# Rows of x sent straight to their expert's places, without a token table

## The chip, the cores and the metric

One core of a Trainium2 chip runs the kernel. It has five engines that run their own instruction lists in order: TensorE (matmuls), VectorE, ScalarE, GpSimd and SyncE (DMA issues only). The metric is the device time of one execution in microseconds (us), lower is better. The clock of TensorE is granted in two levels, 1.2 and 2.4 GHz; the profile gives the share of full speed in each stretch.

## What is computed

A linear attention (8 batches, 8 heads, 576 positions, 64 wide) feeds a mixture of experts with one expert for each token (4608 tokens, 512 wide, 8 experts, hidden width 1024).

```python
def _attn_ref(q, k, v):
    q_s = np.exp(q - np.max(q, axis=-1, keepdims=True))
    q_s = q_s / (np.sum(q_s, axis=-1, keepdims=True) + 1e-09)
    k_s = np.exp(k - np.max(k, axis=2, keepdims=True))
    k_s = k_s / (np.sum(k_s, axis=2, keepdims=True) + 1e-09)
    kv = np.einsum('bhsd,bhse->bhde', k_s, v)
    return np.einsum('bhsd,bhde->bhse', q_s, kv)
def _moe_ref(x, expert_emb, tau, w1, w2):
    # xn, en: rows of x and expert_emb divided by their norm
    logits = xn @ en.T / tau
    expert_idx = np.argmax(logits, axis=1)
    # gate_w: softmax of the logits at expert_idx
    for e in range(E):
        mask = expert_idx == e
        h = np.maximum(x[mask] @ w1[e], 0.0)
        out[mask] = gate_w[mask, None] * (h @ w2[e])
```

x is the attention's result with positions as rows and heads side by side.

## The kernel before

The work goes in four groups of two batches (g = 0 to 3; 1152 tokens, nine tiles of 128). A group's attention has named steps: loads `lk`, `lv`, `lq` (1152 KB each, two of each in a group, on SyncE's queue); the maximum over k (`mx`, `pT`, `mcol`, `mc`, `pB`, `mb`), subtraction `ks`, exponential `ke`; `von` and `vc` copy v beside a column of ones on ScalarE; `kv0` to `kv3` multiply k and v on TensorE; `rs`, `kvx`, `kvd`, `pkT`, `kvT`, `pG`, `cG` make the matrix that gives x and the expert logits at once. For q there are the maximum `qm`, the subtraction `qs` on GpSimd, and for each tile the transposes `pE`, exponential `ec`, matmul `px`, and `ra`, `rr`, `xm`, `lm`, `sq`, which leave x in SBUF and the logits.

Routing goes in five parts, a to e: group 0 in two (a: five tiles, b: four), the others whole. `r`, `pr`, `s` (prefix z for b) find each token's expert and its place among that expert's tokens (`posu`); `gA` to `gE` give the gate. Each expert owns 4608 places. A table in DRAM of 8 bytes for each place holds the token's number and gate: it is first filled with an out-of-range number (`cP`, L266 to L268: a memset on GpSimd, a DMA on SyncE ahead of all loads), and each tile's 128 entries are scattered into it (`sc0` to `sc8`, an indirect DMA on GpSimd, L705). x goes to DRAM in token order by two stores for each group (`st0`, `st1`, L603), and its first five tiles once more for slot 0 (`sta`, L615).

Tokens are processed in slots, each for one expert. Six early slots (256 tokens) run between the attention steps: slots 0 and 1 after parts a and b, slots 2 to 5 after part c, planned by `ya`, `yb`, `yc` on VectorE. The rest are late slots (384 tokens), planned by `lp` and run in a loop under conditions that the device evaluates. A slot loads its stretch of the table (`ix`, SyncE, L931), masks numbers past its end (`im`, VectorE, L1073), gathers its rows of x by these numbers (`xg`, an indirect DMA on GpSimd for every 128 rows, L936), transposes them (`x..p`, `x..h`, `x..l`), runs the two layers (`pa`, `pb`, `hh`, `hl`, `po`, `ob`; each operand split into a high and a low part, so three matmuls for each product) and scatters the result to `out` (`od`, L1018). Slot 0 doesn't read the table: `first_ids` (`fo`, `fp`, `fi`) makes its numbers by a one-hot comparison on VectorE and a matmul, and it gathers from the copy of L615.

`ORDER` is one list of all steps, written out: each engine issues its instructions in this order and waits where an operand is late. `room` and `load` give the tiles for k, v, q: group 0 has its own on the left; later groups have one each for k0, k1, ve0, ve1 and two in turn for v and q on the right. The tile of x holds first q less its maximum, then x.

Of the kernel before, what the change touches and what calls it, by code (L numbers as in the profile page):

```python
# [12 lines left out]
I32 = mybir.dt.int32  # L13
# [16 lines left out]
KX = D + E + 1  # L30
TS = 3
T = TS * P
CAP = N
SENT = E * CAP
TROWS = SENT + T
# [25 lines left out]
PAD_LEFT, PAD_RIGHT = 88, 176  # L61
# [10 lines left out]
cP.0 enL.0 lk0.0 lk1.0 lv0.0 lq0.0 lq1.0 kvP.0 lv1.1 cV.0 lk0.1 von0.1 lv1.0 von1.1 von1.0 von0.0 lk1.1 lv0.1 mx00.0  # L72
mx01.0 enA.0 mx02.0 mx03.0 pT0.0 mx10.0 mcol0.0 mx11.0 mc0.0 pB0.0 enV.0 vc0.0 ks00.0 enP.0 enC.0 ke00.0 mx12.0
qm0.0 kv0.0 mx13.0 kv1.0 qs00.0 qm1.0 pT1.0 qs01.0 vc1.1 mcol1.0 qs11.0 mc1.0 lq0.1 pB1.0 qs10.0 ks10.0 vc1.0 pE0.0
mx00.1 pE2.0 mx01.1 pE1.0 mx02.1 ke10.0 mx03.1 mx10.1 ec2.0 kv2.0 mx11.1 ec1.0 ec0.0 mx12.1 pT0.1 kv3.0 vc0.1
mcol0.1 mx13.1 pT1.1 left.4 rs.0 mcol1.1 kvd.0 lq1.1 kvx.0 mc0.1 pkT.0 qm0.1 pB0.1 kvT.0 mb0.1 pG.0 mc1.1 ks01.1
pB1.1 cG.0 pE3.0 ks10.1 px1.0 px2.0 qs00.1 ec3.0 pE5.0 ra1.0 ra2.0 pE6.0 rr1.0 ke10.1 rr2.0 xm1.0 pE4.0 ks00.1 lm2.0
xm2.0 lm1.0 px3.0 sq1.0 qm1.1 px0.0 ec4.0 qs01.1 ra3.0 pE7.0 ke00.1 rr3.0 xm3.0 qs10.1 lv1.2 lm3.0 ec6.0 px4.0 ec7.0
pE8.0 ra0.0 ra4.0 rr0.0 qs11.1 sq3.0 rr4.0 xm0.0 ec5.0 xm4.0 sq2.0 lm4.0 sta.0 lm0.0 px6.0 sq0.0 r0.0 lv0.2 px7.0
sq4.0 r1.0 st0.0 r2.0 ra6.0 pE0.1 gA.0 r3.0 ec8.0 rr6.0 r4.0 pE2.1 ra7.0 xm6.0 ec0.1 pE1.1 r5.0 sq6.0 rr7.0 pr.0  # L80
lm6.0 xm7.0 px8.0 s0.0 sq7.0 lm7.0 s1.0 px5.0 gB.0 ec1.1 s2.0 gC.0 ra8.0 ra5.0 rr8.0 gD.0 s3.0 rr5.0 ec2.1 s4.0
# [10 lines left out]
w2h03.4 pb03.4 mcol1.2 st0.1 hl02.4 sq4.1 px7.1 rr5.1 hh03.4 xm5.1 w2l03.4 w202.4 x1p1.4 ra7.1 hl03.4 sq5.1 x1p0.4
rr7.1 pB0.2 lm5.1 x1h1.4 lm7.1 px8.1 xm7.1 x1h0.4 w200.4 mb0.2 x1l1.4 px6.1 sq7.1 ks01.2 x1l0.4 ra8.1 ra6.1 rr8.1
pa13.4 mc1.2 rr6.1 lm8.1 xm6.1 xm8.1 sq6.1 pa10.4 ks00.2 lm6.1 st1.1 sq8.1 r0.1 w2h02.4 pb13.4 r1.1 w2h00.4 gA.1
w2l02.4 pB1.2 pb10.4 ke00.2 w2l00.4 ks10.2 po00.4 qs00.2 ke10.2 r2.1 qs11.2 kv0.2 qs10.2 ob00.4 pa11.4 qs01.2 lv1.3
po01.4 od00.4 gB.1 lv0.3 r3.1 gC.1 r4.1 gD.1 r5.1 gE.1 pb11.4 hh10.4 ob01.4 hl10.4 kv1.2 hh13.4 od01.4 hh11.4 hl13.4
# [5 lines left out]
xm1.2 sq0.2 qm0.3 sq1.2 ec5.2 w1h12.4 im2.4 w1l12.4 pT0.3 xg2.4 w2h11.4 px7.2 im3.4 pT1.3 w110.4 mcol0.3 ra7.2 pE4.2
ob11.4 rr7.2 mcol1.3 px5.2 mc0.3 xm7.2 w2l11.4 pB0.3 lm7.2 sq7.2 pE3.2 ec4.2 px6.2 ra5.2 od11.4 mc1.3 pE8.2 rr5.2
w210.4 mb0.3 lm5.2 ra6.2 xm5.2 x2p1.4 ec3.2 ks00.3 rr6.2 px4.2 sq5.2 lm6.2 xm6.2 x2p0.4 x2h1.4 ra4.2 px3.2 x2l1.4
x2h0.4 ks01.3 rr4.2 ec8.2 pE2.2 x2l0.4 ix4.4 sq6.2 pB1.3 lm4.2 xm4.2 pa23.4 w2h10.4 ks10.3 ec2.2 xg3.4 px8.2 sq4.2
pb23.4 ra3.2 w1h10.4 w2l10.4 pa21.4 ke10.3 w1l10.4 w212.4 pa22.4 im4.4 w213.4 rr3.2 hh23.4 lm3.2 xm3.2 pb21.4 ra8.2
# [12 lines left out]
s1.3 x5l1.4 s2.3 s3.3 lp0.3 s4.3 lp1.3 s5.3 lp2.3 s6.3 lp3.3 sc7.3 lp4.3 lp5.3 lp6.3 lp7.3 sc0.3 lp8.3 lp9.3 x5p0.4
lp10.3 ob40.4 lp11.3 sc4.3 lp12.3 lp13.3 x5h0.4 po41.4 lp14.3 lp15.3 sc6.3 x5l0.4 lp16.3 sc8.3 lp17.3 lp18.3 lp19.3  # L120
lp20.3 sc2.3 lp21.3 lp22.3 lp23.3 lp24.3 od40.4 lp25.3 lp26.3 lp27.3 lp28.3 sc3.3 lp29.3 lp30.3 lp31.3 sc5.3 ob41.4
od41.4 sc1.3 right.4
# [4 lines left out]
def attention_moe(ctx, tc, q, k, v, emb, tau, w1, w2, out):  # L127
# [30 lines left out]
    early_rows = wk.tile([P, EARLY_J, DM], F32, tag="xge", bufs=1, name="xge")  # L158
# [13 lines left out]
    x_scr = dram.tile([N, DM], F32, name="x_scr")  # L172

    NA = ROUTES["a"][2]
    x_a = dram.tile([P * NA, DM], F32, name="x_a")
    table = dram.tile([TROWS, 2], I32, name="table")

# [9 lines left out]

    row = const.tile([P, NT, 2], I32, name="row")
# [52 lines left out]
    def const_steps():  # L241
        s = {}

        def cP():
# [8 lines left out]
            for i in range(2):  # L253
                POOL.iota(part_i[:, :, i], [[0, NA]], base=0, channel_multiplier=(NA - 1, 1)[i])
# [72 lines left out]
    def room(side, what, shape):  # L327

        return att[side].tile(shape, F32, tag=what, name=what)
# [881 lines left out]
```

## Time and profile before

| | us |
|---|---|
| median of 3 runs (lowest, highest) | 649.75 (648.42, 651.2) |
| profiled execution | 644.16 |
| its span, first to last instruction | 642.3 |
| TensorE busy (matmuls) | 561.1 |
| VectorE, ScalarE, GpSimd busy | 336.0, 280.5, 202.4 |
| stores of x for one group; the copy for slot 0 | 1280 KB and 1024 KB; 1280 KB |
| bytes moved by DMA; read from, written to HBM | 109.78 MB; 89.71 MB, 21.04 MB |

The profiled execution is one run with the hardware profiler on. Busy times overlap, so they don't add up to the span. The number behind an instruction in the rows below is its idle time before it, and after the arrow what ended that.

### The profile page before, as it was taken

What the parts mean: (1) busy time and instruction counts of PE and PEld (TensorE: products, weight loads), DVE (VectorE), ACT (ScalarE), POOL (GpSimd) and SP (SyncE); (2) the same over time, 40 slices, a digit from 0 to 9 for tenths busy, and PEclk for the clock granted to TensorE, in tenths of its full rate; (3) what the DMA queues carried; (4) which work ended last, traced back from release to release, by engine and by line L of the source; (5) the groups of instructions that cost most, each with busy time, mean ns of one, the idle gap of its engine ahead of it and who ended that gap; (6) DMA issues with size and microseconds to landing.
All of it is one profiled execution on the core that took longest, in us unless ns stands there. A gap on an engine that the chain in (4) does not pass through costs nothing. (4 is left out here: it accounts for less than half of the span.)

```text
span 642.3 us, 13299 instructions
## 1 busy us (share of the span) xinstructions
PE 561.1 (87%) x5178; PEld 501.3 (78%) x5178; DVE 336.0 (52%) x569; ACT 280.5 (44%) x420; POOL 202.4 (32%) x194
## 2 busy tenths in 40 slices
PE   0467658996989895999799999999999999999995
PEld 0356547885869784888699989889989898989894
DVE  4977548972968822262245365652536252544440
ACT  2568345732568143221345355552534353434440
POOL 3417260965163724126320302203030211213111
PEclk9997768997979996999899999999999999999999
DMA  6984992845846100321794567755464555554100
GB/s 214 391 299 175 330 282 58 311 165 167 275 135 247 51 19 2 132 84 34 262 294 129 167 191 238 229 166 186 134 194 134 181 180 164 181 182 139 63 23 29
DMA packets 65859, 109.78 MB, mean 171 GB/s; under 512 B 10702, under 2 KB 35310, under 8 KB 64624
## 3 DMA queue, kind: packets, MB, share of 16 engines
q1 hardware_dynamic: 58144, 89.74, 42.9%
q0 software_dynamic: 7552, 18.92, 8.6%
q8 instruction: 51, 0.84, 0.6%
q14 instruction: 32, 0.26, 0.1%
q10 hardware_dynamic: 80, 0.02, 0.0%
HBM read 89.71 MB, written 21.04 MB: 172 GB/s over the span
## 5 line engine op out<-in xcount | busy, mean ns | idle before, releaser
L1018 POOL DMA_INDIRECT out_dram<-ob,ix x38 | 39.4, 1037 | 288.6 <-ACT ob L1016 248.2
L993 PE MATMUL ph<-x,w1h 128*128 128x384 f32 (+1 forms) x320 | 102.2, 319 | 2.2 <-ACT ob L1016 1.2
L995 PE MATMUL ph<-x,w1l 128*128 128x384 f32 (+1 forms) x320 | 102.1, 319 | 0.0
L994 PE MATMUL ph<-x,w1h 128*128 128x384 f32 (+1 forms) x320 | 102.0, 319 | 0.0
L961 DVE TENSOR_TENSOR w2l<-r,w2h 128x1024 fp32r<-128x1024 f32 x44 | 54.6, 1242 | 73.6 <-ACT w2h L959 73.6
L1011 PE MATMUL po<-w2h,h_l 128*128 128x512 f32 x224 | 88.8, 396 | 0.1
L1012 PE MATMUL po<-w2l,h_l 128*128 128x512 f32 x224 | 87.7, 391 | 0.0
L1013 PE MATMUL po<-w2h,h_l 128*128 128x512 f32 x224 | 87.6, 391 | 0.0
L1016 ACT ACTIVATE ob<-po,ix 128x512 f32<-128x512 f32 x38 | 26.2, 688 | 128.5 <-PE po L1013 64.4
L999 DVE SCALAR_TENSOR_TENSOR h_l<-ph,h_l 128x768 fp32r<-128x768 f32 (+1 forms) x44 | 37.9, 861 | 75.2 <-ACT h_l L997 73.1
L961 DVE TENSOR_TENSOR w1l<-r,w1h 128x1024 fp32r<-128x1024 f32 x48 | 56.8, 1219 | 28.5 <-ACT w1h L959 25.3
L997 ACT ACTIVATE h_l<-ph 128x768 fp32r<-128x768 f32 (+1 forms) x44 | 32.3, 734 | 87.2 <-issue 64.0
L993 PEld LDWEIGHTS ph<-x,w1h 128*128 128x128 f32 x320 | 60.4, 189 | 3.3 <-ACT ob L1016 1.6
L994 PEld LDWEIGHTS ph<-x,w1h 128*128 128x128 f32 x320 | 60.5, 189 | 0.3
L995 PEld LDWEIGHTS ph<-x,w1l 128*128 128x128 f32 x320 | 60.5, 189 | 0.0
L993 PE MATMUL ph<-x_e,w1h 128*128 128x256 f32 x192 | 57.4, 299 | 1.0 <-ACT et L550 0.7
L994 PE MATMUL ph<-x_e,w1h 128*128 128x256 f32 x192 | 55.5, 289 | 0.2
L995 PE MATMUL ph<-x_e,w1l 128*128 128x256 f32 x192 | 55.4, 288 | 0.2 <-issue 0.2
L959 ACT CAST w2h<-r 128x1024 fp32r<-128x1024 f32 x48 | 50.1, 1043 | 4.2 <-ACT ob L1016 1.2
L959 ACT CAST w1h<-r 128x1024 fp32r<-128x1024 f32 x48 | 48.4, 1051 | 5.6 <-DMA r<-in_moe_w_dram 5.6
L1013 PEld LDWEIGHTS po<-w2h,h_l 128*128 128x128 f32 x224 | 42.3, 189 | 9.0
L1011 PEld LDWEIGHTS po<-w2h,h_l 128*128 128x128 f32 x224 | 42.4, 189 | 8.8 <-issue 0.3
(274 smaller groups left out, 1057.7 us busy)
## 6 DMA issues: line engine op xcount, KB each, us to landing
r<-in_moe_w_dram SPq DMA_DIRECT2D x96, 512.0 KB
k<-in_k_dram SPq DMA_DIRECT2D x8, 1152.0 KB
v<-in_v_dram SPq DMA_DIRECT2D x8, 1152.0 KB
q<-in_q_dram SPq DMA_DIRECT2D x8, 1152.0 KB
x_scr<-x SPq DMA_DIRECT2D x4, 1280.0 KB
x_scr<-x SPq DMA_DIRECT2D x4, 1024.0 KB
x_a<-x SPq DMA_DIRECT2D x1, 1280.0 KB
out_dram<-ob,ix POOLq DMA_INDIRECT x38
```

The lines of the kernel that those rows point to most:

```text
L959: ACT.copy(hi, src)
L961: eng.tensor_tensor(lo, src, hi.bitcast(F32), ALU.subtract)
L993: PE.matmul(o, w1h[c][:, d, fs], xh[:, d, :n], start=d == 0, stop=False)
L994: PE.matmul(o, w1h[c][:, d, fs], xl[:, d, :n], start=False, stop=False)
L995: PE.matmul(o, w1l[c][:, d, fs], xh[:, d, :n], start=False, stop=d == NC1 - 1)
L997: ACT.activation(hh[c][:, :, :n], ph[:, :, :n], AF.Relu)
L999: DVE.scalar_tensor_tensor(hl[c][:, :, :n], ph[:, :, :n], 0.0, hh[c][:, :, :n].bitcast(F32), ALU.max, ALU.subtract)
L1011: PE.matmul(po, hh[c][:, u, ts_], w2h[c][:, u, :], start=c + u == 0, stop=False)
L1012: PE.matmul(po, hh[c][:, u, ts_], w2l[c][:, u, :], start=False, stop=False)
L1013: PE.matmul(po, hl[c][:, u, ts_], w2h[c][:, u, :], start=False, stop=c + u == NC2 // 2)
L1016: ACT.activation(ob, po, AF.Copy, scale=ix[:, j, 1:2].bitcast(F32))
L1018: ins = POOL.indirect_dma_start(out, bass.IndirectOffsetOnAxis(ap=ix[:, j, 0:1], axis=0), ob, None, bounds_check=N - 1, oob_is_err=False,)
```

## The change

The table, its first filling, the stores of x in token order, the copy for slot 0 and `first_ids` are removed. A row of x in SBUF gets two words more (`DX` = 514): the token's number (`xi`, one iota for each group) and its gate (written by `gE`). `sc` now scatters these whole rows of 2056 bytes, 128 at a time, to their expert's places in DRAM (`x_by_e`), as many scatters as before. Since a slot's tokens then lie one after another, the plan computes row numbers from a start and a count (`place`, `over`), the slot gathers with them directly, and two VectorE instructions (`numbers`, step `im`) take number and gate out of the gathered rows. The late plan spreads its starts and counts over partitions with a matmul (`lq`) and four steps (`lr`). Gathers and scatters are declared independent where a scatter follows a gather; a gather still waits for the scatters before it.

k, v, ve, q of groups 1 to 3 share six places in turn (`RING`, the one whose last user stands earliest in `ORDER`), and for groups 2 and 3 q less its maximum has two of these places (`qd`) instead of x's tile. `ORDER` is written anew: its beginning, the stretch around slot 0's gather (before, `xg0.4` stood behind four scatters of part a) and that of group 1's scatters now read

```
cP.0 enL.0 lk0.0 lk1.0 lq1.0 lv0.0 lq0.0 xi.0 lv1.0 cV.0 kvP.0 lk0.1 lv1.1 von0.0 von1.0 xi.1 lk1.1 lv0.1 mx00.0
...
ya11.0 w1h02.4 zs3.0 lm2.1 zs4.0 sc0.0 mx10.2 zs5.0 w1h00.4 mx11.2 yb0.0 w1l00.4 zs6.0 w103.4 yb1.0 sc8.0 rr0.1
xm2.1 lm0.1 sc7.0 px7.1 sq2.1 xm0.1 qm0.2 px3.1 sq0.1 sc5.0 ra7.1 ec8.1 sc6.0 ra3.1 pE5.1 ec6.1 qm1.2 w1h03.4 pE4.1
w1l03.4 xg0.4 mx12.2 w203.4 rr7.1 mx13.2 xm7.1 hroom.4 lm7.1 sq7.1 yb2.0 px8.1 mcol0.2 yb3.0 mc0.2 w1l02.4 pT1.2
ra8.1 ec4.1 rr8.1 w2h03.4 w200.4 pB0.2 im0.4 mcol1.2 lm8.1 x0p0.4 mb0.2 w2l03.4 xm8.1 mc1.2 x0p1.4 x0h0.4 rr3.1
...
s6.1 yc3.1 sc3.1 mx10.3 lq1.3 yc4.1 mx11.3 sc8.1 pa12.4 ob01.4 yc5.1 mx12.3 hh11.4 sc6.1 pb13.4 yc6.1 hl11.4 od01.4
yc7.1 mx13.3 w110.4 pb12.4 sc1.1 hh13.4 w111.4 yc8.1 yc9.1 yc10.1 hl13.4 sc7.1 pT0.3 hh12.4 yc11.1 pa10.4 mcol0.3
sc2.1 hl12.4 mc0.3 qm1.3 sc0.1 pT1.3 pkT.2 sc4.1 pb10.4 kvT.2 sc5.1 mcol1.3 pB0.3 hh10.4 pG.2 mc1.3 hl10.4 mb0.3
w1h10.4 pB1.3 ks00.3 cG.2 po10.4 ks10.3 w1h11.4 ks01.3 ke10.3 xi.2 w1l11.4 xg2.4 ke00.3 pE1.2 w1l10.4 w211.4 pE3.2
```

The diff's core:

```diff
+DX = DM + 2
-SENT = E * CAP
-TROWS = SENT + T
+ROWS = E * CAP
+RING = 6
-    x_scr = dram.tile([N, DM], F32, name="x_scr")
-    x_a = dram.tile([P * NA, DM], F32, name="x_a")
-    table = dram.tile([TROWS, 2], I32, name="table")
+    x_by_e = dram.tile([ROWS, DX], I32, name="x_by_e")
...
-            oob = wk.tile([P, TROWS * 2 // P], I32, tag="lh", bufs=1, name="oob")
-            POOL.memset(oob, OOB)
-            SP.dma_start(table.rearrange("(p f) o -> p (f o)", p=P), oob)
...
+    def room(g, what, shape, users):
+        if not g:
+            return att["left"].tile(shape, F32, tag=what, name=what)
+        done = {i: max((emitted[x] for x in old), default=-1) for i, old in enumerate(ring) if emitted.keys() >= set(old)}
+        i = min(done, key=done.get)
+        ring[i] = [f"{x}.{g}" for x in users]
...
         def qs(u, i):
-            if u + i == 0:
-                buf["x", g] = room("right" if g else "x0", "x", [P, GT, DM])
+            if i == 0 and g >= 2:
+                s["qd", u] = room(g, f"qd{u}", [P, GT, 2, P], [f"pE{j}" for j in range(GT)])
+            elif i == 0:
+                s["qd", u] = x_of(g)[:, :, :DM].rearrange("p j (b c x) -> p b j c x", b=2, c=2)[:, u]
...
+        def xi():
+            POOL.iota(x_of(g).bitcast(I32)[:, :, DM], [[1, GT]], base=2 * g * S, channel_multiplier=GT)
...
-            DVE.reciprocal(row[:, cs, 1].bitcast(F32), col("gs"))
+            DVE.reciprocal(buf["x", g][:, j0:j1, DM + 1], col("gs"))
...
             ins = POOL.indirect_dma_start(
-                table,
+                x_by_e,
                 bass.IndirectOffsetOnAxis(ap=posu[:, c : c + 1], axis=0),
-                row[:, c, :],
+                buf["x", g][:, j].bitcast(I32),
                 None,
...
+            tc.declare_no_dep(ins.ins, group="gather", reason="rows that no part routed before has")
...
+            lambda: DVE.scalar_tensor_tensor(place, number_q, val[:, 1:2], over, ALU.add, ALU.max),
...
+        def spread():
+            b["t"] = ps.tile([P, 2, n], F32, tag="t", name="spread")
+            PE.matmul(b["t"], ones[:n, :], start_count, start=True, stop=True)
...
+        chain(NG - 1, "lr", [
+            lambda: DVE.tensor_tensor(over, number_n, b["ct"], ALU.is_ge),
+            lambda: DVE.tensor_scalar(over, over, float(OOB), None, ALU.mult),
+            lambda: DVE.tensor_tensor(place, number_n, b["st"], ALU.add),
+            lambda: DVE.tensor_tensor(place, place, over, ALU.max),
+        ])
...
-        def places():
...
-            SP.dma_start(ix[:, :nt], table[ds(st, nt * P), :].rearrange("(j p) o -> p j o", p=P).bitcast(U32))
         def tokens():
             for j in range(nt):
...
+                ins = POOL.indirect_dma_start(
+                    xg[:, j].bitcast(I32), None, x_by_e, bass.IndirectOffsetOnAxis(ap=place[:, i, j : j + 1], axis=0),
+                    bounds_check=ROWS - 1, oob_is_err=False,
                 )
+        def numbers():
+            DVE.tensor_tensor(ix[:, :, 0], xg.bitcast(U32)[:, :, DM], over[:, i], ALU.max)
+            DVE.tensor_copy(ix[:, :, 1].bitcast(F32), xg[:, :, DM + 1])
...
-    first_ids()
```

## Rows read from the trace of the kernel before

**Rows 1.** Stretches of the span: busy time of each engine, granted clock, DMA share, GB/s.
```profile
0.00:20.00 20.00, 1.94 (x8) 1.07 (x8) 10.55 (x24) 5.80 (x7) 5.62 (x41) 1.00 0.71 249
20.00:40.00 20.00, 9.66 (x209) 8.37 (x212) 16.67 (x18) 11.71 (x10) 8.68 (x4) 1.00 1.06 391
80.00:100.00 20.00, 11.77 (x141) 9.68 (x138) 9.46 (x32) 8.95 (x15) 10.31 (x10) 0.59 1.00 269
...
0.00:320.00 320.00, 248.07 (x3459) 215.72 (x3460) 190.07 (x431) 143.00 (x256) 141.31 (x140) 0.90 0.54 181
320.00:640.00 320.00, 313.01 (x1720) 285.58 (x1719) 145.93 (x138) 137.49 (x165) 61.08 (x54) 1.00 0.51 162
```

**Rows 2.** SyncE's DMA queue, 0 to 8 us: start, us, line, tensors, [idle before].
```profile
5.21 0.39 SPq L268 DMA_DIRECT2D table<-oob  x1
5.65 1.03 SPq L341 DMA_DIRECT2D k<-in_k_dram  x2
```

**Rows 3.** ScalarE's DMA queue, 0 to 8 us.
```profile
0.82 1.58 ACTq L289 DMA_DIRECT2D en<-in_moe_expert_emb_dram  x4
```

**Rows 4.** ScalarE in order of time, 15 to 40 us.
```profile
34.45 2.11 ACT L432 COPY ve<-v 128x2304 f32<-128x2304 f32 x1 [4.65 <-DMA v<-in_v_dram]
36.47 2.12 ACT L418 ACTIVATE k<-k 128x2304 f32<-128x2304 f32 x1
```

**Rows 5.** VectorE in order of time, 10 to 36 us.
```profile
30.58 2.55 DVE L413 TENSOR_TENSOR k<-k,pB 128x2304 f32<-128x2304 f32 x1 [1.29 <-PE pB L401]
```

**Rows 6.** TensorE in order of time, 30 to 50 us.
```profile
38.64 2.23 PE L443 MATMUL pkv<-ve,k 64*64 64x65 f32 x72 [3.08 <-ACT k L418]
```

**Rows 7.** GpSimd in order of time, 75 to 120 us.
```profile
83.48 1.06 POOL L936 DMA_INDIRECT xge<-x_a,ids_a  x1 [0.30 <-issue]
...
95.05 0.97 POOL L705 DMA_INDIRECT table<-row,posu  x1 [0.30 <-issue]
...
114.99 1.26 POOL L936 DMA_INDIRECT xge<-x_scr,ix  x1 [0.31 <-PE ph L995]
```

**Rows 8.** TensorE, 88 to 98 us.
```profile
94.20 1.09 PE L979 MATMUL pt<-ident,xge 128*128 128x128 f32 x4 [5.09 <-DMA xge<-x_a,ids_a]
```

**Rows 9.** TensorE, 118 to 120 us.
```profile
118.97 1.06 PE L979 MATMUL pt<-ident,xge 128*128 128x128 f32 x8 [0.32 <-DMA xge<-x_scr,ix]
```

**Rows 10.** VectorE, 88 to 92 us.
```profile
90.74 0.17 DVE L680 CAST posu<-posb 128x4 uint32<-128x4 f32 x1
```

**Rows 11.** Groups by line and shape, whole span: count | busy us, mean ns | idle before.
```profile
L705 POOL DMA_INDIRECT table<-row,posu x36 | 37.0, 1027 | 30.3 <-issue 10.0 <-DVE rq L576 5.8 <-DVE p_tiles L829 5.4
...
L560 PE MATMUL px<-kvx,et 64*64 64x73 f32 x1152 | 30.5, 255 | 10.8 <-ACT et L550 7.4 <-ACT k L418 1.6 <-DVE lh L589 1.2
...
L546 PE MATMUL pE<-ident,x 128*128 128x128 f32 x144 | 27.8, 343 | 3.3 <-POOL x L536 2.2 <-ACT et L550 0.9 <-DVE x_e L961 0.2
...
L1073 DVE TENSOR_TENSOR ix<-ix,e_over 128x2 uint32<-128x2 uint32 x6 | 3.0, 502 | 0.0
...
L774 DVE TENSOR_TENSOR xge<-places,rel 128x1280 bf16<-128x1280 f32 x1 | 1.5, 1487 | 0.0
```

**Rows 12.** DMA rate in 40 equal slices of 285 to 303 us.
```profile
GB/s 0 0 0 0 0 0 0 0 0 2 0 0 2 0 0 2 0 1 2 0 2 1 0 2 0 0 255 328 0 2 0 0 2 0 0 0 0 0 0 146
```

**Rows 13.** SyncE's DMA queue, 300 to 318 us.
```profile
307.21 0.39 SPq L931 DMA_DIRECT2D ix<-table  x1
```

**Rows 14.** GpSimd, 300 to 318 us.
```profile
309.87 1.05 POOL L936 DMA_INDIRECT xg<-x_scr,ix  x1 [3.55 <-DMA ix<-table]
```

**Rows 15.** TensorE, 314 to 320 us.
```profile
316.94 1.09 PE L979 MATMUL pt<-ident,xg 128*128 128x128 f32 x4 [2.93 <-DMA xg<-x_scr,ix]
```

**Rows 16.** Waits of the whole span: who waited for whom, us, times, longest.
```profile
ACT kvd L468 <- remote: 9.9, 1, 9.9
...
PE px L560 <- ACT et L550: 7.4, 1, 7.4
...
PE pkT L473 <- ACT kvd L468: 3.7, 3, 2.8
```

More of the change, by code (lines that the diff above doesn't have):

```diff
@@ L71 @@
 ORDER = """
[L72 to L81, printed above, removed]
@@ L92 @@
[L92 to L96, printed above, removed]
@@ L102 @@
[L102 to L106, printed above, removed]
@@ L122 @@
-od41.4 sc1.3 right.4
+cP.0 enL.0 lk0.0 lk1.0 lq1.0 lv0.0 lq0.0 xi.0 lv1.0 cV.0 kvP.0 lk0.1 lv1.1 von0.0 von1.0 xi.1 lk1.1 lv0.1 mx00.0
+mx01.0 enA.0 mx02.0 mx03.0 pT0.0 mx10.0 mcol0.0 mx11.0 mc0.0 pB0.0 enV.0 ks00.0 enP.0 mx12.0 ke00.0 enC.0 mx13.0
+qm1.0 pT1.0 vc0.0 mcol1.0 kv0.0 qs10.0 qm0.0 mc1.0 pB1.0 kv1.0 qs11.0 vc1.0 ks10.0 qs00.0 ke10.0 mx00.1 qs01.0 kv2.0
+kv3.0 von1.1 mx01.1 vc1.1 mx02.1 pE2.0 rs.0 pE0.0 mx03.1 kvd.0 lq1.1 pE1.0 kvx.0 ec0.0 ec1.0 mx10.1 pkT.0 ec2.0
+pT0.1 mx11.1 kvT.0 mcol0.1 pG.0 von0.1 mx12.1 mc0.1 vc0.1 pB0.1 mx13.1 pE3.0 cG.0 pT1.1 mb0.1 px1.0 lq0.1 mcol1.1
@@ L325, in attention_moe @@
     buf = {}
[L327 to L340 removed]
+    ring = [[] for _ in range(RING)]
+    emitted = {}
+    def room(g, what, shape, users):
[4 more added lines that the diff above has]
+        ring[i] = [f"{x}.{g}" for x in users]
+        n = 1
+        for x in shape[1:]:
+            n *= x
+        t = att["right"].tile([P, GT * HH * (D + 1)], F32, tag=f"ring{i}", name=f"{what}_{g}")[:, :n]
+        return t.rearrange("p (a b c) -> p a b c", a=shape[1], b=shape[2])
+    def load(n, g, u):
+        t = buf[n, g, u] = room(g, f"{n}{u}", [P, HH, GT, D], {
+            "k": [f"kv{2 * u}", f"kv{2 * u + 1}"], "v": [f"vc{u}"], "q": [f"qs{u}{i}" for i in range(2)]
+        }[n])
         SP.dma_start(
@@ L882, in w_room @@
         x_room(m, "e", EARLY_T)
-        xg_t["e"] = [early_rows[:, j] for j in range(EARLY_J)]
+        xg_t["e"] = early_rows
     def hidden_room():
@@ L898, in late_room @@
             x_room(m, i, T)
-            t = m.tile([P, TS, DM], F32, name=f"xg_{i}")
+        for i in range(2):
+            t = m.tile([P, TS, DX], F32, name=f"xg_{i}")
             POOL.memset(t, 0.0)
-            xg_t[i] = [t[:, j] for j in range(TS)]
+            xg_t[i] = t
+        POOL.memset(m.tile([P, PAD_LATE], F32, name="pad_late"), 0.0)
         raws.append([m.tile([P, NC1, FC], F32, name=f"r1_{c}") for c in range(NF)])
@@ L909, in tiles_of, with fetch @@
         return EARLY_J if s < EARLY else TS
-    def fetch(s, par, i, rows, ids=None):
+    def fetch(s, plan, i):
+        par, (place, over) = plan[:2]
         nt = tiles_of(s)
-        ix, xg = ix_t[s % 3], xg_t[set_of(s)]
-        if s < EARLY:
-            r1, r2 = [None] * NF, [None] * NF
-        else:
-            r1, r2 = raws
+        ix, xg = ix_t[s % 3][:, :nt], xg_t[set_of(s)]
+        r1, r2 = [[None] * NF, [None] * NF] if s < EARLY else raws
         def expert():
@@ L1065, in early_fetch @@
         if s not in gots:
-            g = ROUTES[POINTS[q][0]][0]
-            rows, ids = (x_scr[: (g + 1) * 2 * S], None) if s else (x_a, ids_a)
-            gots[s] = fetch(s, plans[q][0], i, rows, ids)
+            gots[s] = fetch(s, plans[q], i)
         gots[s][4][what](*cs)
-    def mask(s, q, i):
-        ids = gots[s][0][:, :EARLY_J, 0]
-        DVE.tensor_tensor(ids, ids, plans[q][1][:, i * EARLY_J : (i + 1) * EARLY_J], ALU.max)
     def lo_engine(kind):
@@ L1145, in attention_moe @@
                 with late(i + 1):
-                    gn = fetch(nxt, par1, i + 1, x_scr)
-                    for part in gn[4][:3]:
-                        part()
+                    gn = fetch(nxt, plans[-1], i + 1)
+                    gn[4][0]()
+                    gn[4][2]()
             def hidden(nt):
```

218 lines of the change are left out of this document (83 added, 135 removed).

## Prediction

> **What bounds the kernel now.** I read the stretches first [rows 1]. From 320 us on TensorE is busy 313 of 320 us at full clock: this is the loop over late slots, and nothing in it that the change touches is waited for. Before 320 us it is busy 248 of 320 us: 72 us idle, and a mean clock of 0.90. So the change can win or lose only in the first 320 us, by moving the chain of loads, attention, routing and first slots. Within it I looked at what ends TensorE's idle stretches. In the first 20 us TensorE works 1.9 us: loads have not landed. At 80 to 100 us it works 11.8 us at clock 0.59 with the DMA engines at 1.00: it waits for slot 0's rows.
>
> **Start.** SyncE's first load of k stands behind the write of the empty table, which waits for the memset of `oob` late in GpSimd's constant work: the table's write goes out at 5.21 and k at 5.65 [rows 2]. ScalarE, which waits for nothing, issues its first DMA at 0.82 [rows 3]. The table, its memset and its write are removed, and `lk0.0` then waits for nothing that I can find. Bounds: 0 (something else holds SyncE) and 5.65 - 0.82 = 4.8 us; I take 4.8, because the nearest row is a free queue's first issue. The loads start beside the small loads of `emb` (ScalarE's queue); if these get late, `enV` holds VectorE ahead of `ks00`; inside the range.
>
> **Order of loads.** k1's exponential starts at 36.47 because the copy of v1 stands before it on ScalarE and v1 landed only at 34.45 [rows 4]; its own input, VectorE's subtraction, was done at 30.58 + 2.55 = 33.13 [rows 5]. TensorE's second half of kv waits for that exponential [rows 6]. In the new order v1 is the sixth load, not the eighth: two loads of 1.18 MB at 391 GB/s [rows 1] are 6.0 us. v1 is then copied before the subtraction ends, and the exponential starts with it: 36.47 - 33.13 = 3.3 us more. Together 8.2 us. The price: q1 stands third, so v0 is one load (3.0 us) later, less than the 4.8 won. The six shared places free later loads earlier or later by little; I take 0 for them, with the wait for slot 0 below as its bound.
>
> **Slot 0.** Before, its rows are gathered from a plain copy of x by numbers that a one-hot product makes; no scatter is needed. The first gather is issued at 83.48, its issue ends at 84.54 [rows 7], and the transposes start at 94.20 after 5.1 us of idle TensorE [rows 8]: 9.7 us to land, with the DMA engines full. A quieter one: issue ended 114.99 + 1.26 = 116.25 [rows 7], transposes at 118.97 [rows 9], at most 2.7 us. Now the gather stands behind all nine scatters of group 0, waits until they have landed, and these need the places of part b, known at 90.74 [rows 10]. Take 8.2 off, and the 1.5 us of the one-hot comparison on VectorE [rows 11]: 81.0. Four scatters at 0.97 + 0.30 us [rows 7] are 5.1: 86.1. A landing L, 1.4 us of gather, a second L: 87.5 + 2L. Meanwhile the new order puts three more `pE` (27.8/36 = 0.77 us each) and three more `px` (30.5/36 = 0.85 each) [rows 11] ahead of these transposes: 4.9 us of work that need not be done later. Against 94.20 this gives 94.2 - (87.5 + 2L - 4.9) = 11.6 - 2L: with L = 2.7 a gain of 6.2 us, with L = 9.7 a loss of 7.8, even at L = 5.8. I take the quiet end: the two stores to x_scr and the copy x_a, 3.7 MB, leave SyncE's queue for 2.4 MB of scatters, and its loads stand 8 us earlier.
>
> The scatters themselves: 36 before and 36 now, 1.03 us each [rows 11], the issue being GpSimd's. That a row has 2056 B instead of 8 shows nowhere yet; the nearest is a scatter of 128 rows of 2 KB to `out`, which moves in two slices of 0.45 us at 255 and 328 GB/s [rows 12], less than the 1.27 us to the next issue. So I price them at 0 on GpSimd, at L in the chain.
>
> Against this speaks the Trainium skill, "DMA: Bandwidth & Descriptors", section "Issuing engines are not separate DMA queues": transfers issued by SyncE and GpSimd run on the same 16 engines, so moving x from one queue to the other buys no bandwidth. The trace agrees so far that a gather took 9.7 us beside full engines. The same page of the Trainium skill, section "Anatomy of one DMA", gives about 2.0 us as the fixed cost of a DMA; as L that would make the gain 7.6, an estimate. The sum goes by the rows.
>
> **x in SBUF.** The tile of x is now held until its nine scatters have read it; `xi.2` and `xi.3` on GpSimd wait for that, and behind them stand `xg2` and `qs00.3`. Price: one landing, 2.7 us, hidden by the FFN matmuls of slots 1 and 3 that the order puts there; without cover 2 x 2.7 of loss. `qd` in places of its own lets `pE.2` run before; taken as 0.
>
> **Small work.** The mask (0.50 us [rows 11], six times) is replaced by two VectorE instructions for each of 16 slots: at 0.50 each 13 us more over the span, on an engine idle 174 us of the second 320 [rows 1]. Each waits for its gather, as the mask did for its table load; behind the first stand `mcol1.2`, `lm8.1` and group 1's rest. Six more VectorE steps and a matmul in the late plan are under 3.5 us at the same price, beside nine scatters of 11.4 us on GpSimd.
>
> **Late slots.** The table load is issued at 307.21 [rows 13], GpSimd waits 3.55 us for it [rows 14], and TensorE 2.93 us for these rows at 316.94 [rows 15]. The load is gone: I take 2.9, bounds 0 (the weights, which land at the same time, end the wait instead) and 3.6. In later slots the same load is hidden: 0.
>
> **Sum.** 6.2 + 2.9 = 9.1 us. The profiled execution took 644.16 us (span 642.3 and 1.9 around it), so 635.1; its own time stands 5.6 below the median of the runs shown, and from the median 649.75 the forecast is 640.7, own range 636 to 646.
>
> **Rivals.** *The bursts stop stalling.* During the long bursts of table scatters ScalarE waited 9.9 us for something not recorded, and TensorE 7.4 us for ScalarE at one place and 2.8 at the other [rows 16]. If rows of 2 KB, or other work beside them, end that, 10.2 us more go: 630.5. For it: the new order puts FFN matmuls beside the bursts. Against: as many scatters as before, and the burst of group 3 shows no such wait. A rule that would make it so is in the Trainium skill, "DMA: Bandwidth & Descriptors", section "Specifications": below 512 B the engines read, modify and write. No row shows what was waited for.
>
> *Slot 0 eats the start.* With L near 5.8 the first gain is gone and 2.9 stays; or x's tile costs its 2.7 twice besides (646.1 alone). 646 to 650, say 648.
>
> *Slot 0 comes later.* Scatters of 263 KB meet loads and both landings take 9.7: 7.8 - 2.9 = 4.9 us lost, 654.7. For it: DMA at 1.00 in that stretch. Against: fewer bytes, started earlier. It decides from L = 7.3 on.
>
> *The start is not moved* (SyncE held otherwise): 4.8 less, 645.5, within the first case's edge.
>
> **Chances.** Forecast 0.52, bursts 0.18, eaten 0.14, later 0.16. Range 628 to 654: from the bursts' price and a little to the later case. Half a per cent, 3.2 us, is about what a measurement of this kernel can tell from no change; 646.5 to 653.0 counts as same. Faster 0.70 (first two), same 0.14, slower 0.16.
>
> **What would show it.** SyncE's first k load near 0.8 us and VectorE's first maximum as much earlier; k1's exponential right behind its subtraction near 28; slot 0's transposes near 93 with little idle before them; no wait for rows at the first late slot; 313 us of TensorE from there on. Wrong if: the gather of slot 0 lands over 5.8 us after its scatters, VectorE stops at `im0`, or a burst of scatters leaves TensorE idle for longer than 7 us.

## The result, and the profile after

The kernel after takes 631.29 us (629.1 to 635.32, 4 runs), the kernel before 649.09 (647.64 to 651.2, 4 runs): ratio 0.973, 95% interval 0.9669 to 0.9792, 17.8 us less. The forecast was 9.1 us less (640.7, range 628 to 654). The direction holds and the time lies in the range, but below the 636 to 646 that the forecast gave itself; the gain is nearly twice the forecast. The profiled execution of after took 632.8 us (span 630.9), 11.4 less than that of before, so the two traces can account for 11.4 of the 17.8 us.

Where the 11.4 us come from is read from the stretches of TensorE, first after, then those of before that [rows 1] does not have. Columns: stretch, its length, busy time (matmuls), granted clock, DMA share, GB/s.

```profile
0.00:40.00 40.00, 19.13 (x414) 0.96 0.92 336
40.00:60.00 20.00, 13.93 (x374) 0.57 0.63 214
60.00:80.00 20.00, 13.42 (x266) 0.81 0.84 282
80.00:100.00 20.00, 10.32 (x116) 0.50 0.46 154
100.00:240.00 140.00, 122.90 (x1642) 0.93 0.49 157
240.00:260.00 20.00, 19.59 (x306) 1.00 0.06 24
260.00:300.00 40.00, 37.18 (x295) 0.96 0.46 145
300.00:320.00 20.00, 20.00 (x115) 1.00 0.79 271
308.00:628.00 320.00, 313.25 (x1732) 1.00 0.49 158
```

```profile
40.00:60.00 20.00, 15.39 (x343) 0.83 0.42 146
60.00:80.00 20.00, 14.41 (x421) 0.76 0.95 339
100.00:240.00 140.00, 126.79 (x1796) 0.94 0.49 158
240.00:260.00 20.00, 12.19 (x208) 0.74 0.02 2
260.00:300.00 40.00, 39.61 (x267) 1.00 0.25 93
300.00:320.00 20.00, 16.32 (x102) 0.90 0.59 200
320.00:325.00 5.00, 5.00 (x19) 0.70 1.07 374
```

Busy time times clock is about the work done. At 40 us after leads by 18.4 - 11.6 = 6.8 us. At 100 us nothing of that is left (42.3 in both). From 100 to 240 it loses 4.9. At 240 to 260 it wins 10.6, where TensorE before works 12.2 of 20 us. From 260 to 300 it loses 3.9, from 300 to 320 it wins 5.3, the wait at the first late slot and slow matmuls behind it. That makes 7.1 us by 320. Most of the rest comes while the first late slot of before still runs below full clock (0.70 from 320 to 325): from its transposes to the next slot's it takes 27.0 us (316.94 to 343.91), in after 23.5 (308.66 to 332.12). So on this account the gain comes from two places, and the start is neither of them. From the second late slot on the loop is as before: 313 of 320 us, as forecast.

The start itself came as forecast. SyncE's queue, ScalarE and TensorE of after, against [rows 2, 4, 6]: the first k load 4.8 us earlier, k1's exponential right behind its subtraction and 11.6 us earlier, the second half of kv (in one piece now) 11.5 us earlier where 8.2 were forecast.

```profile
0.81 0.99 SPq L325 DMA_DIRECT2D k<-in_k_dram  x2
```

```profile
24.87 2.12 ACT L402 ACTIVATE k<-k 128x2304 f32<-128x2304 f32 x1 [1.21 <-DVE k L397]
```

```profile
27.10 3.49 PE L427 MATMUL pkv<-ve,k 64*64 64x65 f32 x144 [2.69 <-issue]
```

Slot 0 of after, all engines in order of time, against [rows 7, 8, 10]: scatters of part a from 71.94, of part b to 90.68, the gather that waits for their landing, VectorE's `im0` (L905) that waits for the rows, behind it `mcol`, behind that TensorE's transposes.

```profile
71.94 1.20 POOL L689 DMA_INDIRECT x_by_e<-x,posu  x1 [0.20 <-DVE e_val L729]
...
77.27 0.97 POOL L689 DMA_INDIRECT x_by_e<-x,posu  x1 [0.30 <-issue]
77.81 0.27 ACT L569 ACTIVATE rq<-px,tiny 128x8 f32<-128x8 f32 x1 [7.16 <-remote]
...
85.44 0.17 DVE L664 CAST posu<-posb 128x4 uint32<-128x4 f32 x1
...
89.71 0.97 POOL L689 DMA_INDIRECT x_by_e<-x,posu  x1 [0.30 <-issue]
90.21 0.27 ACT L569 ACTIVATE rq<-px,tiny 128x8 f32<-128x8 f32 x1 [2.27 <-remote]
...
94.47 1.30 POOL L897 DMA_INDIRECT xge<-x_by_e,e_place  x1 [3.78 <-DMA x_by_e<-x,posu]
...
96.07 1.16 POOL L897 DMA_INDIRECT xge<-x_by_e,e_place  x1 [0.31 <-issue]
...
102.00 0.72 DVE L905 TENSOR_TENSOR ix<-xge,e_over 128x2 uint32<-128x2 uint32 x1 [2.90 <-DMA xge<-x_by_e,e_place]
```

```profile
97.28 1.25 PE L556 MATMUL px<-kvx,et 64*64 64x73 f32 x32 [3.47 <-DVE lh L585]
...
103.19 1.97 PE L947 MATMUL pt<-ident,xge 128*128 128x128 f32 x8 [3.09 <-DVE mcol L357]
```

The transposes start at 103.19, not at 93. And the first late slot, GpSimd and TensorE, against [rows 14, 15]: no wait for rows.

```profile
302.04 1.05 POOL L897 DMA_INDIRECT xg<-x_by_e,late_place  x1 [0.17 <-POOL pad_late L872]
```

```profile
308.66 1.47 PE L947 MATMUL pt<-ident,xg 128*128 128x128 f32 x12
```

The 10.6 us at 240 to 260 us are the second wait of [rows 16]. This is the kernel before there, all engines:

```profile
238.99 0.74 PE L560 MATMUL px<-kvx,et 64*64 64x73 f32 x32
...
246.99 0.97 POOL L705 DMA_INDIRECT table<-row,posu  x1 [0.30 <-issue]
248.05 0.27 ACT L573 ACTIVATE rq<-px,tiny 128x8 f32<-128x8 f32 x1 [7.81 <-remote]
248.27 0.97 POOL L705 DMA_INDIRECT table<-row,posu  x1 [0.31 <-issue]
...
250.20 1.47 PE L560 MATMUL px<-kvx,et 64*64 64x73 f32 x32 [7.37 <-ACT et L550]
```

ScalarE's `rq` needs the `px` that ended at 239.73 and starts at 248.05. It resumes between the eighth and the last of nine scatters, and TensorE waits for what ScalarE does next. "remote" is the profile's word for a wait that ends with nothing it has a record of. I call this holding: while GpSimd issues scatters without a pause, a signal from one engine reaches another late, near the end of the burst. It is not gone in after: two waits of ScalarE above end with a burst of group 0, and the bursts of groups 1 and 3 come with such waits of 6.4 to 10.5 us. But at group 2's burst no wait ends so, and TensorE has matmuls of a slot's layers to do. TensorE beside that burst in after, then before, in the columns above:

```profile
216.40:227.80 11.40, 11.40 (x76) 1.00 0.60 222
...
238.00:249.30 11.30, 4.28 (x56) 0.79 0.04 3
```

### The profile page after: what moved, and what is told of

It is laid out like the page before. It is cut to its first block, busy times and chain, and to the rows that moved or that the text cites. A ratio compares the mean times of both kernels' runs of the same rounds, so it can differ in the third digit from the quotient of the medians.

```text
span 630.9 us, 13218 instructions
## 1 busy us (share of the span) xinstructions
PE 557.7 (88%) x5170; PEld 500.1 (79%) x5170; DVE 325.9 (52%) x594; ACT 278.9 (44%) x420; POOL 201.7 (32%) x192
## 5 line engine op out<-in xcount | busy, mean ns | idle before, releaser
L556 PE MATMUL px<-kvx,et 64*64 64x73 f32 x1152 | 35.3, 265 | 21.7 <-DVE lh L585 6.2
L556 PEld LDWEIGHTS px<-kvx,et 64*64 64x64 f32 x1152 | 28.7, 163 | 30.3 <-issue 13.1
```

The source lines that it names most:

```text
L556: PE.matmul(s["px", j][o, i, n * KX : (n + 1) * KX], s["et", j][r, 2 * b + c, h * D : (h + 1) * D], kvx_t[g % 2][r, b, c, h, :], start=Tru ...
```

## The experiments

Theories. A, the prediction's: start, order of loads, slot 0 and late slots make the gain. B, its rival: bursts stop stalling. Those that came up later (D, that slot 0's rows come late and cost time, among them) are stated in the expectations. Runs that stand in one block of the table (one number under "before") shared a chip and its runs of before. The record gives the chips of the five blocks as 5, 5, 15, 4 and 0.

| | edit | us | before | ratio (95%) |
|---|---|---|---|---|
| e1 | before again | 645.68 | 645.38 | 1.000 (0.9965, 1.0035) |
| e2 | before, start | 641.93 | | 0.9916 (0.9879, 0.9953) |
| e3 | after, no start | 633.82 | | 0.9782 (0.9735, 0.983) |
| e4 | before, group 2's scatters apart | 637.93 | | 0.9853 (0.9798, 0.9908) |
| e5 | after again | 626.03 | 626.33 | 0.9979 (0.9947, 1.0012) |
| e6 | before, e2 and e4 | 622.4 | | 0.9929 (0.9897, 0.996) |
| e7 | after, late landing | 621.53 | | 0.9923 (0.9892, 0.9954) |
| e8 | after, im later | 625.36 | | 0.9977 (0.9945, 1.0009) |
| e9 | before again | 646.86 | 645.96 | one run |
| e10 | after again | 629.65 | | 0.9739 (0.969, 0.9787) |
| e11 | after, slot 0's gather earlier | 633.16 | | 0.9798 (0.9744, 0.9852) |
| e13 | before, group 2's scatters moved | 642.34 | 645.34 | 0.9935 (0.9904, 0.9965) |
| e14 | after, groups 0 and 1 apart | 647.87 | | 1.0057 (1.0029, 1.0085) |
| e15 | after, late landing | 631.14 | | 0.9766 (0.9712, 0.9821) |
| e17 | before, e2 and e4 | 632.93 | 644.41 | 0.9795 (0.9758, 0.9833) |
| e18 | e17, v1 sixth | 635.99 | | 0.9822 (0.9765, 0.988) |

**The kernels unchanged (e1, e5, e9, e10).**

> The kernel before, unchanged, for a second trace. Its profiled execution (644.16 us) stood 5 us below its timed runs (647.6 to 651.2). If that was one quick execution, the second profile takes 647 to 651 us and one of its waits before 320 us is 3 to 7 us longer than in the first trace; if the profiler itself makes the kernel quicker, the second profile takes 644 us again. Timed ratio 1.00.

> The kernel after, unchanged, for a second trace and more runs on a chip with many runs of the kernel before: 630 to 633 us, ratio to before 0.976 to 0.980 (the 19 runs of before beside the first four experiments had a median of 645.4, not 649.1). If the first comparison had it right, ratio 0.973.

> The kernel before, unchanged, for a trace beside the runs that follow. On the chip of the first four experiments each trace holds waits of 5 to 10 us that end with a burst of scatters; on the chip of the next four no trace holds one. If this chip is of the first kind: 645 us, ScalarE's wait at group 2's burst 8 to 10 us. If of the second: 626 us, no such wait, and the time that the change saves is then under 2 us.

> The kernel after, unchanged. On a chip that holds signals during bursts: ratio to before 0.973 to 0.980. On one that does not: 0.995 to 1.001. Nothing between.

e1's profiled execution took 642.61 us, e9's 646.86: one kernel's executions spread over 641 to 650 us. Both traces have the wait at group 2's burst (9.8 and 6.6 us). e5 is the surprise: in its block before takes 626.3 and after 626.0. In none of the traces of e5 to e8 does a wait end with "remote"; in the kernels' traces of all the other blocks, and of the first comparison, some of 5 to 13 us do. So the change gains 2.6% (e10) where signals are held and nothing that can be measured where they are not. Expecting 0.976 or 0.973 in e5 was wrong; what was expected of the two kinds of chip in e9 and e10 held. But that the kinds are kinds of chip is not shown: the block of e5 to e8 has the same chip number, 5, as that of e1 to e4. I can only say that blocks differ.

The two kinds of block differ in their records as well. Of 241 DMAs the trace of e5 has 3797 landing records and that of after 3208; of 267, e6 has 4236 and before 3689. The list of DMAs, which gives a median time from issue to landing in e5, has none in after:

```profile
x_by_e<-x,posu POOLq DMA_INDIRECT x36, 5.0
...
x_by_e<-x,posu POOLq DMA_INDIRECT x36
```

e12's trace, in a block that holds, lacks landing records too without a held turn. Each run that the record lists has a granted clock beside its time, so none is known to have gone unrecorded. Whether recording takes part in the holding is a rival that no run tests.

**Start alone (e2, e3).**

```diff
-            SP.dma_start(table.rearrange("(p f) o -> p (f o)", p=P), oob)
+        def tb():
+            SP.dma_start(table.rearrange("(p f) o -> p (f o)", p=P), s["oob"])
-... lk0.0 lk1.0 lv0.0 lq0.0 lq1.0 kvP.0 ...
+... lk0.0 lk1.0 lv0.0 lq0.0 lq1.0 tb.0 kvP.0 ...
```

e3 puts into `cP` of after a memset of a 128 x 576 tile and `SP.dma_start(table..., oob)`, ahead of the loads.

> The kernel before with one edit: the write of the empty table goes behind the fifth load on SyncE's queue, so that the first load waits for nothing. Theory A (the prediction's start term is carried to the end): the first load near 0.8 us and 4.8 us less in the end, ratio 0.9926. Theory B (what the start wins is lost again at later waits of the first 100 us, above all at slot 0's rows): group 0's first matmuls 4.8 us earlier, 0 to 2 us less in the end, ratio 0.997 to 1.000.

> The kernel after with one edit: a memset late in GpSimd's constant work and a 288 KB write of it to DRAM stand ahead of SyncE's loads again. Theory A: the first load near 5.6 us and 4.8 to 5.6 us more than the kernel after, so near 636.5 us, ratio to before 0.981. Theory B: 0 to 2 us more, 631 to 633 us, ratio 0.973 to 0.976.

On the kernel before, the start is carried to the end: 0.84%, 5.4 us by the ratio (3.5 by the medians). TensorE's row in e2 that answers to [rows 6] is 5.1 us earlier:

```profile
33.58 2.23 PE L445 MATMUL pkv<-ve,k 64*64 64x65 f32 x72 [3.20 <-ACT k L420]
```

On the kernel after, with the first load at 4.78 us instead of 0.81, the time is 2.5 us more (633.82 against 631.29 of another block; 0.5% by the ratios). That stands between A and B, and the intervals overlap: how much of the term gets through the new order is not settled.

**Group 2's burst (e4, e13).** e4 puts memsets between the scatters of before; e13 moves these scatters, back to back, to where after has them.

```diff
             tc.declare_no_dep(ins.ins, group="scatter", reason="own places")
+            if c // GT in THIN:
+                for _ in range(6):
+                    POOL.memset(pads[0], 0.0)
```

```diff
-... rr4.3 sc1.2 px8.3 ... sc0.2 ec7.3 ... sc8.2 ra0.3 ec1.3 rr0.3 sc2.2 ...
+... s6.2 sc1.2 sc0.2 sc4.2 sc6.2 sc5.2 sc3.2 sc7.2 sc8.2 sc2.2 ...
```

> The kernel before with six memsets of a small pad tile (about 1 us together) behind each of group 2's nine scatters on GpSimd. Theory B (back-to-back scatters hold the signals of other engines; the burst of group 2 at 238 to 249 us made ScalarE wait 7.8 us and TensorE 7.4 us, and half of the gain of the change is that this is gone): with the scatters apart ScalarE's wait there is under 2 us and 7 to 10 us go, ratio 0.985 to 0.990. Theory A: nothing changes by over 0.5%, the wait was chance or something other than the spacing.

> The kernel before with group 2's nine scatters moved in ORDER from between group 3's px steps to right behind s6.2, as the kernel after has them, beside the matmuls of a slot's layers. Theory B (on a chip that holds signals the change wins there by where the burst stands): ScalarE's wait of 7 to 10 us no longer stops TensorE, 6 to 10 us less than before, ratio 0.985 to 0.991, as with the memsets. If it is the spacing alone that helps: within 2 us of before.

Spacing gives 1.5% (7.4 us by medians, 9.5 by the ratio), though GpSimd works 10 us more (six memsets take 1.3 us): ScalarE's wait is gone, and TensorE's longest between 200 and 300 us is 1.9. Theory B holds for its place and price. The move alone gives 0.65%, 4.2 us by the ratio (3.0 by the medians, of runs from 639 to 652 us), between its two expectations. The burst holds signals at its new place as well, but TensorE's wait is shorter than the 7.37 us of before. ScalarE's held wait there, and behind it TensorE's, which needs that `kvd`:

```profile
230.10 0.58 ACT L468 COPY kvd<-pkv 128x512 f32<-128x512 f32 x1 [12.88 <-remote]
230.75 1.11 PE L473 MATMUL pkT<-ident,kvd 128*128 128x128 f32 x4 [4.38 <-issue]
```

**Both on the kernel before (e6, e17; e18 with another order of loads).** e18 exchanges `lv1.1` and `lv1.0` in ORDER.

> The kernel before with both edits that won: the table's write behind the fifth load, and group 2's scatters apart by 1 us of memsets. If the two gains lie in different places they add: 0.9916 times 0.9853 is 0.977, 630 to 632 us, as fast as the kernel after without its change. If the start's gain was carried only because the burst then falls elsewhere, less than 1% below the better of the two alone: 635 to 638 us.

> The kernel before with the write of the empty table behind the fifth load and memsets between group 2's scatters (as e6), for a chip that holds signals. If the change's whole gain there is these two things: ratio to before 0.972 to 0.980 (0.9916 times 0.9853 is 0.977), like the kernel after's 0.973 and 0.974. If the change wins by something else as well: 0.982 or more. On a chip that does not hold them: 0.993 again.

> As e17, and group 0's v1 is the sixth transfer of the start and group 1's v1 the eighth, as in the kernel after. Prediction's order term: k1's exponential starts with its subtraction, 3.3 us earlier, and 3.3 us less than e17 in the end (0.5%). Rival (what is won there is lost at later waits of the first 100 us): the exponential earlier, the end within 1 us of e17.

Where signals are held (e17), two small edits, which keep the table, give 2.05% of the change's 2.6% to 2.7%; the intervals overlap. Where they are not (e6), they give 0.7%, no more than the start alone does in e2. Their median is 3.6 us below that of the kernel after in the same block (622.4 against 626.0). That the rest of the change costs so much there is not shown: the intervals just overlap, and e7, the kernel after with one small DMA more, took 621.5. e18 missed its aim: ScalarE still copies group 1's v1 first, so the exponential came 4.4 us later than in e17 (31.41 us there), not 3.3 earlier, and the end moved by less than the intervals. The order term is not tested by it. ScalarE in e18:

```profile
30.04 2.11 ACT L438 COPY ve<-v 128x2304 f32<-128x2304 f32 x1 [11.76 <-DMA v<-in_v_dram]
...
35.84 2.13 ACT L424 ACTIVATE k<-k 128x2304 f32<-128x2304 f32 x1 [1.36 <-DVE k L419]
```

**Slot 0 of the kernel after (e8, e11, e14).** e8 moves each `im` behind the splits of x; e11 moves the gather ahead of part b's scatters; e14 is e4's edit with `THIN = (0, 1)`, so that slot 0's gather comes later.

```diff
-... pB0.2 im0.4 mcol1.2 ... x0l0.4 x0h1.4 ...
+... pB0.2 mcol1.2 ... x0l0.4 im0.4 x0h1.4 ...
```

```diff
-... yb1.0 sc8.0 rr0.1 ... w1l03.4 xg0.4 mx12.2 ...
+... yb1.0 xg0.4 sc8.0 rr0.1 ... w1l03.4 mx12.2 ...
```

> The kernel after with ORDER alone changed: each early slot's step im (VectorE takes number and gate out of the gathered rows) stands behind that slot's splits of x instead of ahead of its transposes. If VectorE's stop at im0 (2.9 us, and TensorE 3.1 us behind it) is why slot 0 came late and cost the early gain: 2 to 4 us less, 627 to 630 us. If the scatters' chain itself sets slot 0: within 1 us of the kernel after.

> The kernel after with one step moved in ORDER: slot 0's gather stands between part a's five scatters and part b's four, so that it waits for the five alone. Theory D (the early gain of 6.2 us that was forecast is lost because the chain of nine scatters and two landings makes slot 0 come at 102 instead of 93 us): the rows land near 86, VectorE no longer stops at im0, and 3 to 6 us less than the kernel after. Rival (group 1's attention is as late as slot 0, VectorE's order being what holds both): within 1.5 us of the kernel after.

> The kernel after with 1 us of memsets behind each scatter of groups 0 and 1. If the waits at the bursts of group 0 (7.2 and 2.3 us of ScalarE at 71 to 91 us) are what ate the early gain: 2 to 5 us less than the kernel after (ratio to before 0.966 to 0.971 on a chip that holds signals). If it is the order of VectorE's work: no gain, 0 to 3 us more, since slot 0's gather comes 8 us later.

e8 changes nothing in the median (625.36 against 626.03), in a block that holds nothing. Its profiled execution (620.82 us) has slot 0's transposes at 94.49, that of e5 (626.13 us) at 101.92. e11 has the rows long before they are needed, the gather going out at 83.76; the transposes come at 100.97 anyway, and the time is 633.2 against 629.7, no better. But ScalarE's longest held wait at part a's burst is 8.6 us there and 5.2 in e10, so the bursts are still in it. In e14 the gather goes out at 100.32, 5.9 us later than in after, TensorE is idle for 16.7 us, and the time is 647.9 against e15's 631.1.

```profile
83.76 1.56 POOL L897 DMA_INDIRECT xge<-x_by_e,e_place  x1 [6.25 <-DVE e_cnt L739]
...
100.97 1.48 PE L947 MATMUL pt<-ident,xge 128*128 128x128 f32 x8
```

```profile
110.66 1.97 PE L954 MATMUL pt<-ident,xge 128*128 128x128 f32 x8 [16.65 <-DVE mcol L361]
```

So theory D falls as put: earlier rows win nothing (e11). What later rows cost, e14 can't say alone: slot 0's transposes come 7.5 us later than in after, slot 2's 18.0 (194.20 against 176.17), and group 1's scatters, spaced by the same edit, stand between.

**The late landing (e7, e15).**

```diff
         def tokens():
+            if s == EARLY:
+                SP.dma_start(xg[:, 0, :TS].bitcast(U32), place[:, i])
```

> The kernel after with one DMA more: ahead of the first late slot's gathers SyncE copies 12 bytes for each partition of that slot's row numbers into the tile that the gathers then fill, so that GpSimd waits for a landing there as it did for the table load. Prediction's late term: 2.9 us more, 634 to 635 us. Theory C (behind such a wait TensorE's clock is granted at half for some 7 us as well, so the wait costs twice its length): 4 to 6 us more. If the wait is covered: within 1 us of the kernel after.

> The kernel after with the 12-byte copy ahead of the first late slot's gathers, again, for a chip that holds signals. Prediction's late term: 2.9 us more than the kernel after, ratio to before 0.978 to 0.979; with the clock at half behind the wait 4 to 6 us more, 0.981 to 0.984; covered: 0.973 to 0.975.

e15 is 1.5 us over e10 and 0.2 under the first 631.29; its interval reaches into all three expectations, so the trace has to decide: its transposes (12 at 308.96) start with no idle time before them. e7 came out 4.5 us faster than e5, which no theory expects; its trace is ahead from 97 us on, long before the edit, and I can't say why. A landing more is covered in the new kernel where signals are held. Where they are not, the kernel after comes to this slot 10 us earlier (298.47 in e5) and waits there too, up to 1.46 us for rows; the slot then takes 27.3 us, as in before.

**What holding needs (e12, e16).**

> Not the workload: TensorE and ScalarE hand a 128 x 128 tile to and fro (some 1 us a turn) while GpSimd runs five stages: nine scatters of 8-byte rows in a row, nine of 2056-byte rows, nine of 8-byte rows with 1 us of memsets between, the memsets alone, nine gathers of 2056-byte rows. The output is not the reference's. Theory B on a chip that holds signals: turns of 3 to 10 us in the first two stages, none over 2 us in the third and fourth. If the wait came from the bytes or from writes under 512 B: in one of the first two stages alone. On a chip that does not hold them: turns alike in all stages.

> Not the workload: the ping-pong of e12 with 32 small matmuls of TensorE in each turn instead of one transpose, as dense as the px steps. The output is not the reference's. In e12 the turns were alike in all stages. If signals are held only while TensorE's instructions come fast: on a chip that holds them, turns of 3 to 10 us (against some 2) in the stages of scatters in a row, none in the stage with memsets between or the memsets alone. If they are alike again, it needs something else of the kernel, which stays open.

e12's block was one that holds signals (e9 to e11), and its turns are alike in all five stages; theory B as I had put it, that scatters in a row are enough, falls (e12 and e16 are one execution each). ScalarE's waits for TensorE's turns in e12, of all stages (us in total, times, longest us):

```profile
ACT x L47 <- PE t L45: 82.5, 146, 0.6
```

With 32 matmuls in each turn (e16; the trace has two records for each) ScalarE waits up to 11.6 us for a turn. Its rows in order of time: the stages of 8-byte rows (scatters 17.0 to 28.4), of 2056-byte rows (83.6 to 94.8), with memsets between (one of nine turns alike), and of gathers (192.2 to 203.7); then TensorE in the first two of them.

```profile
28.62 0.27 ACT L51 COPY x<-t 128x128 f32<-128x128 f32 x1 [11.01 <-remote]
...
96.79 0.27 ACT L51 COPY x<-t 128x128 f32<-128x128 f32 x1 [11.61 <-remote]
...
164.26 0.27 ACT L51 COPY x<-t 128x128 f32<-128x128 f32 x1 [2.62 <-PE t L49]
...
195.10 0.27 ACT L51 COPY x<-t 128x128 f32<-128x128 f32 x1 [4.21 <-remote]
205.48 0.27 ACT L51 COPY x<-t 128x128 f32<-128x128 f32 x1 [10.12 <-PE t L49]
```

```profile
19.78 0.50 PE L49 MATMUL t<-x,ident 64*64 64x64 f32 x4 [0.15 <-issue]
28.94 2.19 PE L49 MATMUL t<-x,ident 64*64 64x64 f32 x64 [8.65 <-issue]
...
85.24 0.80 PE L49 MATMUL t<-x,ident 64*64 64x64 f32 x39 [1.55 <-ACT x L51]
...
93.65 0.47 PE L49 MATMUL t<-x,ident 64*64 64x64 f32 x2 [0.93 <-issue]
```

Elsewhere ScalarE waits 1.3 to 2.3 us a turn, beside spaced scatters up to 2.8. In the first stage TensorE's turn is over at 20.28 and ScalarE's copy of it starts at 28.62: the signal is 8.3 us late, and TensorE's 8.65 us are its wait for that copy. In the second TensorE itself is slowed: one turn takes from 85.24 to 94.12, 8.9 us against 1.2 to 2.0 elsewhere, in small pieces with waits for nothing that the profile shows. So here it takes indirect DMAs in a row and a dense stream of TensorE instructions. Small rows, large rows and gathers all do it, and 1.3 us of other GpSimd work between two DMAs is enough to prevent it.

## Why the prediction was wrong in its size

Two steps failed, in opposite directions: slot 0's gain of 6.2 did not come, and the bursts, put at nothing in the sum, were worth about the whole forecast. A third, the late slot, was sized too small.

*Start* (4.8 of 8.2): right. The loads moved by 4.8, and alone the edit is worth 3.5 to 5.4 on the kernel before (e2).

*Order of loads* (3.3): group 0 gained 11.5 instead of 8.2 in all. Whether the order's part reaches the end was not tested (e18).

*Slot 0* (6.2): this step failed. "I take the quiet end" was one part: the scatters' landing took 3.8 and the gather's up to 4.8 us, not 2.7 each. The other parts: the places of part b came 4.4 us later than 81.0, the two gathers took 1.4 longer to issue, and VectorE's `im0` and `mcol` stood ahead of the transposes for 1.2. With 0.1 for the four scatters that is 0.1 + 1.1 + 2.1 + 4.4 + 1.4 + 1.2 = 10.3, and the forecast's 92.9 + 10.3 = 103.2. By 100 us nothing of the early lead was left. But the step was also the wrong gate: e11 brings the rows early and wins nothing. TensorE's longest waits near 100 us are for VectorE's results (3.47 and 3.09 us above), and from 40 to 100 us the granted clock is 0.57, 0.81 and 0.50, against 0.83, 0.76 and 0.59 before. Which of group 0's bursts and VectorE's order is to blame is open: e14 took the bursts' waits away, but moved the gather and group 1's scatters as well.

*The scatters, priced at 0, and the bursts:* the term that was put at nothing in the sum, and the main reason that the forecast was too small. The rival had its place and price (10.2; measured 10.6 in the trace, 7.4 to 9.5 alone in e4), at a chance of 0.18. I held against it that there are as many scatters as before. What counts is what TensorE has to do beside a burst (it was busy 11.40 of 11.40 us in after, 4.28 of 11.30 before), and whether signals are held at all: in the block of e5 the change gains nothing.

The Trainium skill, "DMA: Bandwidth & Descriptors", section "Specifications" (read, modify and write below 512 B), was the rule that I gave for that rival. The runs don't bear it out as the cause: 8-byte and 2056-byte rows hold alike (11.0 and 11.6 us in e16), and gathers too.

*Small work and x in SBUF*, priced at 0: nothing in the runs speaks against it, but they were not tried alone; the 3.6 us between e5 and e6, if they are real, have to lie in them, in the new order or at slot 0.

*Late slots* (2.9): the trace shows 5.3 us from 300 to 320, since the clock is granted at 0.90 there before and 1.00 after: the wait cost its length and slow matmuls behind it. With the rest of that slot it is 6.4 us (2.9 of wait, and 27.0 against 23.5 for the slot), so the term was sized too small. That the table's landing was its cause is not borne out: put back, it is covered (e15). SyncE issues that slot's first weights at 286.56 in after and 308.18 in before; that they no longer share the wires with the gathers is likely and was not tried.

The account by what was measured where signals are held: start and spacing together give 2.05% (e17), 13.2 us, of the 2.6% (e10) to 2.7% of the change. The 0.6% between them, some 4 us, is inside the intervals. The first late slot would cover it: e17 still waits 2.65 us there. Neither edit needs the table gone. The burst is moved by the new `ORDER`, and the start comes from a write that could have stood elsewhere; sending rows straight to their places is not shown to be worth anything by itself.

## What to carry to other kernels

A lead won at the head of a chain counts only if nothing between there and the bound end takes it: follow it stretch by stretch (busy time times clock), and ask of each next stretch what else is late. A long wait with no recorded releaser that ends with a burst of GpSimd's DMAs is a price like any other: space the burst, or put independent matmuls beside it, and see it go. Run both kernels in more than one block of runs before a gain is put down to the change: this one was 17.8 us in one and nothing that could be measured in another, and two edits of a few lines gave most of it.

## What the runs showed of the hardware

In blocks of runs that hold, four of five, indirect DMAs that GpSimd issues 1.28 us apart slow a densely issuing TensorE (8.9 us for a turn, e16) and delay its signals (8.3 us there); ScalarE's waits reach 12.9 us (e13). In one block this doesn't show, and the same two kernels take 626 instead of 645 and 630 us. Why blocks differ is open. The chip's number is 5 in one of either kind, and the traces that show holding lack landing records, so the recording itself is not excluded.

What holds them is open too. The instruction queue moves 79 blocks in e16 and 1 in e12, where nothing is held. In e16 the stretch from 17 to 23 us has this row, those from 23 to 28.6 and from 28.6 to 32.9 have none:

```profile
q8 instruction: 1, 0.02, 1.2%
```

The Trainium skill, "Runtime: NRT & Kernel Launch", section "Instruction fetch mechanics", says that an engine's sequencer fetches its code in blocks of 16 KiB over a DMA queue of its own. The trace agrees on the size (1.29 MB in 79 blocks). TensorE goes on at 28.94 and is through a whole turn before another block moves, so it had its code: the wait in this stage was not for code.
